# Low parts of the first keys moved behind the second minimum, and a second price for the sum of ident's rows

## The chip, the cores and the metric

The kernel runs on one core of a Trainium2 chip. The metric is the device time of one execution in microseconds (us), as the median of several runs. TensorE is called PE here, its weight load PEld, VectorE DVE, ScalarE ACT, GpSimd POOL and SyncE SP; SP issues the loads and stores.

## What is computed

Three stages follow one another: causal attention with a decay from gates, a feed-forward block with SoLU and a layer norm, and a second feed-forward block with squared relu. All arrays are float32. Shapes: 4 batches, 8 heads, 576 positions, head size 64, so 2304 tokens of width 512; inner widths 1024 and 2048.

```python
def _attn_ref(q, k, v, f):
    scores = scale * np.matmul(q, k.transpose(0, 1, 3, 2))
    cum = np.cumsum(np.log(np.clip(f, 0.0001, 1.0)), axis=-1)
    decay = cum[:, :, :, None] - cum[:, :, None, :]
    scores = np.where(causal, -1000000000.0, scores + decay)
    attn = np.exp(scores - np.max(scores, axis=-1, keepdims=True))
    attn = attn / (np.sum(attn, axis=-1, keepdims=True) + 1e-09)
    return np.matmul(attn, v)

def _moe_ref(x, w_in, w_out, g_ln):
    h = x @ w_in
    solu = h * softmax(h)
    ln = (solu - mean(solu)) / np.sqrt(var(solu) + 1e-06) * g_ln
    return ln @ w_out

def _moe2_ref(x, w_in, w_out):
    h = np.maximum(x @ w_in, 0.0)
    return h * h @ w_out
```

## The kernel before

Every product is made from high and low parts: a number is rounded to the matmul's short form (the high part), and what is missing (the low part) is a second operand. So each tile of keys, queries, sums of gates and weights costs a cast for the high part and a subtraction for the low one, on whichever of ACT, DVE and POOL the plan picks.

The attention goes over 20 tiles of up to 128 queries (tiles 0 and 1 are the first two of batch 0), and in each over 8 heads. Heads 0 to 3 take their operands from row half j = 0, heads 4 to 7 from j = 1. For one head: two matmuls give negated scores in a PSUM tile z0 or z1, in turn (line 576; the second matmul takes the low parts and the gate sums); DVE adds the causal mask and takes the row minimum (597, with a second instruction that reads it out); ACT takes the exponential (611); PE transposes it (630); ACT or DVE copies the transposed tile to `pt` (376, 382); and PE multiplies it with the values (650). A z tile is free for the head after the next only when its exponential is done.

What stands before the first minima: the gates are clipped, their logarithms are summed along the positions in two scans on DVE (1575), the sums get a high part on ACT (1606) and a low part on DVE (1609, `low_sums` in the change), and both go to DRAM (`cumd`), from where the keys' tiles fetch them as extra rows (506). Tile 0 takes its own rows straight from SBUF. Lines 510 and 498 make the high and the low part of the keys (`K1`, `K2`), 384 or 378 the scaled queries, 541 their low part. Line 482 (`picks`) fills rows of the query operand `q2` that pick a head's gate sums out of the extra rows: it adds two slices of the identity matrix `ident`, once for each of two buffers i and two halves j. Buffer i = 0 serves even tiles, i = 1 odd ones. Beside this, the weights of the first block are converted: lines 729, 380 or 378, 733, 737, 743 (a sum of whole words, on POOL alone) and 747 (their low part `wil`).

Each operation is entered as a step with `pl.add`: a price in ns for each engine that may do it, a priority (lower goes first) and the keys it reads and writes, from which the plan takes the dependences. `Plan.lay` then lays out all steps in a list by these prices, and the engines run the program in that order; nothing is reordered on the chip. A step marked `port=True` on DVE is laid so that it doesn't run while a POOL step runs, as the plan's prices have it. Up to a planned time of 140 us, gaps on PE are filled with transposes that nobody reads (1706).

Of the kernel before, what the change touches and what calls it, by code (L numbers as in the profile page):

```python
# [27 lines left out]
class Plan:  # L28
# [11 lines left out]
        dve=dict(pe=230, dve=127, act=198, pool=203, dma=1230),  # L40
        act=dict(pe=110, dve=142, act=153, pool=160, dma=1234),
        pool=dict(pe=135, dve=75, act=75, pool=88, dma=1200),
# [17 lines left out]
    def add(self, eng, fn, prio, reads=(), writes=(), take=None, uses=(), late=0, port=False, kind="r"):  # L60

        s = Step()
        s.eng, s.fn, s.prio, s.take, s.no, s.late = eng, fn, prio, take, len(self.steps), late
        deps = {}
        s.uses = tuple(uses) + ((take,) if take else ())
        for k in s.uses:  # L70
            self.users.setdefault(k, []).append(s)
        s.weak, s.port, s.kind = None, port, kind
        for k in reads:
            if k in self.writer:
                deps[self.writer[k].no] = self.writer[k]
            rs = self.readers.setdefault(k, [])
            if k in self.banks or k[0] in ("pp", "hp"):

                if rs and rs[-1].no not in deps:
                    s.weak = rs[-1]  # L80
                    deps[s.weak.no] = s.weak
            rs.append(s)
        for k in writes:
            if k in self.writer:
                deps[self.writer[k].no] = self.writer[k]
            for r in self.readers.get(k, ()):
                deps[r.no] = r
        for k in writes:
            self.writer[k] = s
            self.readers[k] = []  # L90
        deps.pop(s.no, None)
        s.deps = list(deps.values())
        s.succ = []
        for d in s.deps:
            d.succ.append(s)
        s.left = len(s.deps)
        s.rdy = {}
        s.end = None
        self.steps.append(s)
        return s  # L100

    def fill(self, order, ring, a, b, lag, share):
        ident = self.writer["ident"]
# [165 lines left out]
def tile_kernel(ctx: ExitStack, tc: tile.TileContext, q, k, v, f, w_in, w_out, g_ln, w2_in, w2_out, out):  # L269
# [23 lines left out]
    HH = H // 2  # L293
# [150 lines left out]


    vslot = {}

    def load_k(n, prio):
        T = tiles[n]
# [26 lines left out]
    def picks(i, j):  # L476

        def fn():
            c = D + HH * j
            a, b = (ident[AUX, x : x + HH].unsqueeze(2).broadcast_to([2 * H, HH, P]) for x in (c, c + H))  # L480
            eng = nc.gpsimd if s.on == "pool" else nc.vector
            eng.tensor_tensor(out=Q2[i][j][AUX], in0=a, in1=b, op=ALU.add)

        s = pl.add(dict(dve=602, pool=1252) if i else dict(dve=602), fn, -9.05e6 if i == 0 else 14000, ["ident"], [("qa", i, j)], port=True)

    def prep_k(n, prio):
        T = tiles[n]
# [3 lines left out]
        los = {}  # L491
        for j in range(2):
# [15 lines left out]
            if n == 0 and j:  # L508
# [7 lines left out]
                lo, prio + 2 * j, [("kn", j)] + hk, lk,  # L516
                port=True,
            )
            for y in range(2):
                rk = [f"cumd{y}"] if n else [("c0", 0), ("xh", 0, 0)][y : y + 1]  # L520
                pl.add(
                    dict(dma=350), lambda y=y, auxrows=auxrows: auxrows(y), (prio if n else -7e6) + 2 * j, rk,
                    writes=kcells(f"ka{y}", j, kc, kc + m),
                )

    def prep_q(n, prio):
        m = tiles[n]["m"]
        i = n % 2
        raw = QN[:, 0 : HH * m].rearrange("p (h s) -> p h s", s=m)
        for j, src in enumerate(own):  # L530
            q1, q2 = Q1[i][j], Q2[i][j]
            if n == 0 and j:
                prio = SECOND
            for rows, dst, nm in ((LO, q2, "qh"), (HI, q1, "qd")):
                copy(
                    HH * m, lambda rows=rows, dst=dst: dst[rows, :, 0:m], lambda src=src: raw[src], prio + 2 * j, ["qn"],
                    [(nm, i, j)], (), SC, False, None if n else ("act", "dve")[j:] if j else ("act",),
                )

            def lo(src=src, q1=q1, hi=(q1 if j else q2)):  # L540
                nc.vector.scalar_tensor_tensor(
                    out=q1[LO, :, 0:m], in0=raw[src], scalar=SC, in1=hi[src, :, 0:m].bitcast(F32), op0=ALU.mult,
                    op1=ALU.subtract,
                )

            pl.add(
                dict(dve=67 + 1.045 * HH * m), lo, prio + 2 * j, ["qn", ("qd" if j else "qh", i, j)], [("ql", i, j)],
                port=True,
            )


    def head(s):
# [48 lines left out]

        for y, (c, k_) in enumerate(zip(cuts, zk)):
            w = c[2] - c[1]
            pl.add(
                dict(dve=77 + 1.042 * w + 61 * y), lambda y=y, c=c: least(y, c), prio,
                ["mask"] + [sk_ + (0,)] * y, [k_, sk_ + (y,)],
            )
# [962 lines left out]
    for y, (a, e) in enumerate(((0, P), (P, S))):  # L1570
# [33 lines left out]
        ["mhalf", ("lf", 0), ("lf", 1), ("qh", 0, 0), ("qd", 0, 0)], [("st", 0, 0)],  # L1604
    )
    pl.add(dict(act=573), lambda: nc.scalar.copy(part(0), cu), THIRD, ["cu0", "cu1"], pt0[0])
    pl.add(
        dict(dve=669),
        lambda: nc.vector.tensor_tensor(out=part(1), in0=cu, in1=part(0).bitcast(F32), op=ALU.subtract), THIRD,
        ["cu0", "cu1"] + pt0[0], pt0[1],  # L1610
# [38 lines left out]
    for n in range(NQ):  # L1649
        for h in range(H):  # L1650
# [7 lines left out]
            if h == PQ and n + 1 < NQ:  # L1658
                prep_q(n + 1, when[s])
                if n + 2 < NQ:  # L1660
                    load_q(n + 2, when[s])
            head(s)
            w = 4 if n >= QUADS else 2
            if (h + 1) % w == 0:
                mix(s, w)
# [129 lines left out]
```

## Time and profile before

| | us |
|---|---|
| median of 3 runs | 810.95 |
| lowest and highest | 810.48, 811.85 |
| profiled execution, its own time | 813.03 |
| its span, first to last instruction | 811.2 |

The profile is one execution. 1.83 us of its time lie outside the span. Over the span PE is busy 97%, DVE 79%, ACT 68% and POOL 47%; the granted TensorE clock is 0.998 of its full level, 2.4 GHz. Busy time of PE includes the filling transposes, and ends of matmuls are modelled, so a busy PE is not PE at its peak. A time in a row is the start from the beginning of the span; in square brackets stands the idle time of the engine just before, and what ended it. Rows in which two instructions are grouped give the time from the first one's start to the last one's end.

### The profile page before, as it was taken

The numbers are of one execution on the slowest core, as the hardware profiler recorded it, in microseconds if no ns is written. First come the engines' busy times: TensorE is split into PE (matmuls) and PEld (weight loads), VectorE is DVE, ScalarE is ACT, GpSimd is POOL, SyncE is SP. The second block draws the span as 40 slices with busy tenths as digits, with TensorE's granted clock in tenths as the row PEclk, the third lists the DMA queues.
The fourth block names the chain that finished last, engine by engine and source line by source line (L and its number), as shares of the span: only waits on it lengthen the run. The fifth ranks groups of instructions, "written<-read, shape, count | busy, mean of one in ns | idle before, by whom it ended". The sixth has DMA issues, their size and how long they took to land.

```text
span 811.2 us, 19134 instructions
## 1 busy us (share of the span) xinstructions
PE 790.8 (97%) x6607; PEld 726.7 (90%) x6607; DVE 638.9 (79%) x1627; ACT 550.3 (68%) x1425; POOL 384.6 (47%) x520
## 2 busy tenths in 40 slices
PE   7899999999999999999999999999999999999997
PEld 6677788888888888888989999999999999999997
DVE  8788788787786667886677879779778877987777
ACT  6899998889998888898886775445335343533442
POOL 6467778666778686777757622120211121112110
PEclk9999999999999999999999999999999999999999
DMA  6644346656664555665477899696767767675401
GB/s 216 206 117 140 105 128 186 206 173 190 199 206 163 189 171 165 196 229 180 169 247 232 265 309 368 213 321 212 229 207 233 230 203 223 216 232 186 159 1 53
DMA packets 109665, 159.69 MB, mean 197 GB/s; under 512 B 12832, under 2 KB 52768, under 8 KB 109568
## 3 DMA queue, kind: packets, MB, share of 16 engines
q1 hardware_dynamic: 109280, 158.21, 60.9%
q8 instruction: 52, 0.85, 0.4%
q14 instruction: 45, 0.37, 0.2%
q10 hardware_dynamic: 288, 0.26, 0.1%
HBM read 121.65 MB, written 36.72 MB: 195 GB/s over the span
## 4 chain that ended last, share of the span: by engine, by line
PE 47%; POOL 2%; DVE 2%; issue 1%; DMA 1%; ACT 1%; DVEq 0%; POOLq 0%
PE z L1392 9%; PE pp L1392 9%; PE hp L1497 4%; PE hp L1498 4%; PE hp L1499 4%; PE z L1341 3%; PE xo L1498 2%; PE xo L1499 2%; PE xo L1497 2%; DMA w2d<-free 1%; PE pp L1498 1%; PE pp L1499 1%; PE pp L1497 1%; PE pp L820 1%; PE pp L822 1%
## 5 line engine op out<-in xcount | busy, mean ns | idle before, releaser
L611 ACT ACTIVATE adj<-z,st 64x288 f32<-64x288 f32 (+9 forms) x192 | 95.0, 498 | 17.7 <-DVE st L597 15.9
L576 PE MATMUL z<-k,q 80*64 80x288 f32 (+17 forms) x384 | 89.9, 331 | 0.2
L597 DVE CUSTOM_DVE_ANT_0 z<-z,maskb 128x128 f32<-128x128 f32 (+8 forms) x144 | 65.3, 462 | 26.8 <-PE z L576 24.8
L630 PE MATMUL pp<-ident,adj 128*128 128x128 f32 (+1 forms) x480 | 76.4, 273 | 9.2 <-ACT adj L611 8.2
L821 PE MATMUL pp<-ln,wol 128*128 128x256 f32 x288 | 80.1, 278 | 0.0
L822 PE MATMUL pp<-ln,woh 128*128 128x256 f32 x288 | 80.1, 278 | 0.0
L630 PEld LDWEIGHTS pp<-ident,adj 128*128 128x128 f32 (+1 forms) x480 | 50.7, 140 | 32.4 <-ACT adj L611 22.4
L376 ACT COPY pt<-pp 128x384 f32<-128x384 f32 (+5 forms) x167 | 67.5, 422 | 15.2 <-PE pp L630 13.7
L1153 DVE TENSOR_TENSOR k<-adj,k 128x512 fp32r<-128x512 f32 (+1 forms) x71 | 48.9, 688 | 32.5 <-POOL k L380 25.2
L743 POOL TENSOR_TENSOR free<-free 128x256 uint32<-128x256 uint32 x64 | 49.1, 772 | 33.9 <-DVE free L737 20.7
L576 PEld LDWEIGHTS z<-k,q 128*128 128x128 f32 (+3 forms) x384 | 54.9, 176 | 8.3 <-ACT adj L611 4.1
L869 PE MATMUL hp<-wih,xl 128*128 128x512 f32 x144 | 60.0, 417 | 0.8 <-ACT hp L908 0.8
L650 PE MATMUL xo<-pt,vn 128*64 128x128 f32 (+1 forms) x960 | 60.4, 268 | 0.1
L650 PEld LDWEIGHTS xo<-pt,vn 128*64 128x64 f32 x960 | 48.6, 137 | 9.4 <-issue 5.4
L870 PE MATMUL hp<-wil,xh 128*128 128x512 f32 x144 | 56.6, 393 | 0.2 <-DVE wil L747 0.2
L871 PE MATMUL hp<-wih,xh 128*128 128x512 f32 x144 | 56.8, 394 | 0.0
L1106 POOL TENSOR_TENSOR free<-free 128x256 f32<-128x256 f32 x64 | 52.5, 821 | 7.5 <-DMA w2d<-free 4.8
L821 PEld LDWEIGHTS pp<-ln,wol 128*128 128x128 f32 x288 | 54.4, 189 | 0.4
L822 PEld LDWEIGHTS pp<-ln,woh 128*128 128x128 f32 x288 | 54.1, 188 | 0.0
L1098 POOL TENSOR_TENSOR free<-free 128x256 fp32r<-128x256 f32 x63 | 50.0, 805 | 7.4 <-ACT free L376 6.9
L380 POOL TENSOR_SCALAR k<-adj 128x512 fp32r<-128x512 f32 x37 | 23.1, 624 | 63.7 <-PE xo L1499 25.7
L1392 PE MATMUL z<-wol,k 128*128 128x256 f32 x384 | 52.4, 276 | 0.0
(614 smaller groups left out, 2682.4 us busy)
## 6 DMA issues: line engine op xcount, KB each, us to landing
k<-w2u SPq DMA_DIRECT2D x96, 256.0 KB
ln<-w2u SPq DMA_DIRECT2D x96, 256.0 KB
w2u<-free SPq DMA_DIRECT2D x56, 256.0 KB
kn<-in_k_dram SPq DMA_DIRECT2D x32, 256.0 KB
free<-in_moe_w_out_dram SPq DMA_DIRECT2D x32, 256.0 KB
free<-in_moe_w_in_dram SPq DMA_DIRECT2D x32, 256.0 KB
q<-w2u SPq DMA_DIRECT2D x32, 256.0 KB
w2f<-free SPq DMA_DIRECT2D x49, 128.0 KB
```

What stands on the lines that cost most here:

```text
L376: nc.scalar.copy(dst(), src())
L576: nc.tensor.matmul(dst, lhsT=ql[0:r, p, 0:m], rhs=rhs, start=(g == 0), stop=(g == 1))
L597: nc.vector.tensor_tensor_reduce(out=z, in0=z, in1=maskb[0:m, o : o + e - a], scale=1.0, scalar=st[0:m, 0:1] if y else 3e38, op0=ALU.add, ...
L611: nc.scalar.activation(out=adj[0:m, c[1] : c[2]], in_=Z[c[0]][0:m, 0 : c[2] - c[1]], func=AF.Exp, bias=st[0:m, low : low + 1], scale=-1.0, ...
L630: nc.tensor.transpose(at(sk)[:, (c - g) * m : (c - g + 1) * m], adj[0:m, zc : zc + P], ident[0:m, 0:m])
L650: nc.tensor.matmul(XO[own[j], g // 2, off : off + m], lhsT=VN[vslot[b, c]][:, (g + j) * D : (g + j + 1) * D], rhs=PT[(s - h + g + j) % NPT ...
L821: nc.tensor.matmul(px, lhsT=wol[:, fc, w], rhs=hi, start=False, stop=False)
L822: nc.tensor.matmul(px, lhsT=woh[:, fc, w], rhs=hi, start=False, stop=(fc == KF - 1))
L869: nc.tensor.matmul(HP[:, c], lhsT=XL[i][:, cc, :], rhs=wih[:, cc, w], start=(cc == 0), stop=False)
L871: nc.tensor.matmul(HP[:, c], lhsT=XH[i][:, cc, :], rhs=wih[:, cc, w], start=False, stop=(cc == KC - 1))
L1392: nc.tensor.matmul(half(i), lhsT=l, rhs=r[:, c * TB : c * TB + TB], start=(j == start), stop=(j == 5), skip_group_check=True,)
L1497: nc.tensor.matmul(po, lhsT=gl, rhs=wh, start=(p == 0 and i in opens), stop=False, skip_group_check=True)
```

## The change

Four edits. A function `after` adds a dependence to a step that is already entered. The low part of tile 0's keys of half j = 1 and the low part of the gate sums are made to depend on the minimum of head 1 (`least_of[1, 0]`), that is, the second one. The low part of tile 0's queries of half j = 1 gets priority 9900 where it had 9902. And the price of the sum of ident's rows for buffer i = 1 on DVE goes from 602 to 1500 ns, where POOL's stays at 1252; for i = 0 it stays as it was.

```diff
+    def after(self, s, d):
+        if d not in s.deps:
+            s.deps.append(d)
+            d.succ.append(s)
+            s.left += 1
...
+    held_back, least_of = [], {}
...
-        s = pl.add(dict(dve=602, pool=1252) if i else dict(dve=602), fn, -9.05e6 if i == 0 else 14000, ["ident"], [("qa", i, j)], port=True)
+        s = pl.add(dict(dve=1500, pool=1252) if i else dict(dve=602), fn, -9.05e6 if i == 0 else 14000, ["ident"], [("qa", i, j)], port=True)
...
+            if n == 0 and j:
+                held_back.append(los[j])
...
-            pl.add(
-                dict(dve=67 + 1.045 * HH * m), lo, prio + 2 * j, ["qn", ("qd" if j else "qh", i, j)], [("ql", i, j)],
-                port=True,
+            s = pl.add(
+                dict(dve=67 + 1.045 * HH * m), lo, SECOND if n == 0 and j else prio + 2 * j,
+                ["qn", ("qd" if j else "qh", i, j)], [("ql", i, j)], port=True,
             )
...
-            pl.add(
+            least_of[s, y] = pl.add(
                 dict(dve=77 + 1.042 * w + 61 * y), lambda y=y, c=c: least(y, c), prio,
...
-    pl.add(
+    low_sums = pl.add(
         dict(dve=669),
...
             head(s)
+            if s == 1:
+                for x in held_back + [low_sums]:
+                    pl.after(x, least_of[1, 0])
```

Since the plan is laid step by step, the whole program comes out in another order, on every engine and through to its end; the three places below are at its start. The change's rows carry the line numbers of its own file, which are 6 to 12 higher (482 is 489, 498 is 505, 541 is 550, 597 is 606, 743 is 752, 747 is 756, 1609 is 1618).

DVE between the long scan and the third minimum of tile 0, before and with the change (`k21` is the low part of the keys of j = 1, `q2` and `q101` the queries of j = 1, `free` the gate sums):

```order
L498 TENSOR_TENSOR k21_8_79<-kn1_17_88,k11_46_117 64x4x128
L384 TENSOR_SCALAR q2_20_91<-qn_9_80 64x512
L1609 TENSOR_TENSOR free_21_92<-free_21_92 32x576
L597 ISA z0_121,st0_29_100<-z0_121,maskb_0_71 128x128
L597 ISA st0_29_100 128x1
L597 ISA z1_122,st1_30_101<-z1_122,maskb_0_71 128x128
L597 ISA st1_30_101 128x1
L384 TENSOR_SCALAR q101_42_113<-qn_9_80 64x512
L541 SCALAR_TENSOR_TENSOR q101_42_113<-qn_9_80,q101_42_113 64x512
L597 ISA z0_121,st2_31_102<-z0_121,maskb_0_71 128x128
```

```order
L390 TENSOR_SCALAR q2_20_91<-qn_9_80 64x512
L390 TENSOR_SCALAR q101_42_113<-qn_9_80 64x512
L550 SCALAR_TENSOR_TENSOR q101_42_113<-qn_9_80,q101_42_113 64x512
L606 ISA z0_121,st0_29_100<-z0_121,maskb_0_71 128x128
L606 ISA st0_29_100 128x1
L606 ISA z1_122,st1_30_101<-z1_122,maskb_0_71 128x128
L606 ISA st1_30_101 128x1
L1618 TENSOR_TENSOR free_21_92<-free_21_92 32x576
L505 TENSOR_TENSOR k21_8_79<-kn1_17_88,k11_46_117 64x4x128
L606 ISA z0_121,st2_31_102<-z0_121,maskb_0_71 128x128
```

The two low parts went behind the second minimum, and the second query copy with its low part came ahead of the first.

DVE from the last step of the first weight chunk (L737) to the minima of heads 4 to 7 of tile 0, before and with the change (`k20` and `k21` are here tile 1's keys, `q110` tile 1's queries):

```order
L737 SCALAR_TENSOR_TENSOR ln0_50_209<-ln0_50_209 128x512
L482 TENSOR_TENSOR q2_20_91<-ident_39_110 16x512
L597 ISA z0_121,st0_29_100<-z0_121,maskb_0_71 128x128
L597 ISA st0_29_100 128x1
L597 ISA z1_122,st1_30_101<-z1_122,maskb_0_71 128x128
L597 ISA st1_30_101 128x1
L597 ISA z0_121,st2_31_102<-z0_121,maskb_0_71 128x128
```

```order
L746 SCALAR_TENSOR_TENSOR ln0_50_209<-ln0_50_209 128x512
L505 TENSOR_TENSOR k20_7_78<-kn0_16_87,k10_45_116 64x4x128
L606 ISA z0_121,st0_29_100<-z0_121,maskb_0_71 128x128
L606 ISA st0_29_100 128x1
L606 ISA z1_122,st1_30_101<-z1_122,maskb_0_71 128x128
L606 ISA st1_30_101 128x1
L550 SCALAR_TENSOR_TENSOR q110_43_114<-qn_9_80,q2_20_91 64x512
L606 ISA z0_121,st2_31_102<-z0_121,maskb_0_71 128x128
L606 ISA st2_31_102 128x1
L505 TENSOR_TENSOR k21_8_79<-kn1_17_88,k11_46_117 64x4x128
L606 ISA z1_122,st3_32_103<-z1_122,maskb_0_71 128x128
```

The sum of ident's rows left DVE, and the low parts of tile 1's keys and queries stand between these minima.

POOL in the same stretch, before and with the change:

```order
L482 TENSOR_TENSOR q2_20_91<-ident_39_110 16x512
L380 TENSOR_SCALAR ln0_50_209<-ln0_50_209 128x512
L498 TENSOR_TENSOR k20_7_78<-kn0_16_87,k10_45_116 64x4x128
L498 TENSOR_TENSOR k21_8_79<-kn1_17_88,k11_46_117 64x4x128
L743 TENSOR_TENSOR ln0_50_209<-ln0_50_209 128x512
```

```order
L489 TENSOR_TENSOR q2_20_91<-ident_39_110 16x512
L386 TENSOR_SCALAR ln0_50_209<-ln0_50_209 128x512
L752 TENSOR_TENSOR ln0_50_209<-ln0_50_209 128x512
L756 TENSOR_TENSOR wil_4_75<-ln0_50_209,wih_3_74 128x512
L489 TENSOR_TENSOR q2_20_91<-ident_39_110 16x512
```

POOL gave away both low parts of tile 1's keys, and took the low part of the first weights and the second sum of ident's rows.

## Rows read from the trace of the kernel before

**Rows 1.** Busy us per engine by stretch, then granted clock, DMA share, GB/s.
```profile
0.00:20.00 20.00, 14.72 (x95) 12.51 (x96) 16.25 (x36) 12.26 (x33) 12.84 (x23) 1.00 0.69 216
...
40.00:100.00 60.00, 57.76 (x433) 45.47 (x433) 49.74 (x116) 58.01 (x146) 41.95 (x56) 1.00 0.41 125
...
120.00:440.00 320.00, 314.71 (x2571) 272.15 (x2572) 244.82 (x654) 275.93 (x797) 234.40 (x308) 1.00 0.61 194
440.00:811.00 371.00, 366.57 (x3202) 366.04 (x3200) 296.36 (x747) 166.92 (x348) 72.84 (x109) 1.00 0.66 215
```

**Rows 2.** Instructions of PE in order of time: start, us, line, tiles.
```profile
8.28 0.73 PE L576 MATMUL z<-k,q 128*128 128x256 f32 x4
...
14.41 0.73 PE L576 MATMUL z<-k,q 128*128 128x256 f32 x4
...
18.13 0.68 PE L630 MATMUL pp<-ident,adj 128*128 128x128 f32 x2 [1.84 <-ACT adj L611]
...
26.30 0.66 PE L676 MATMUL pp<-ident,x 128*128 128x128 f32 x4 [1.14 <-ACT x L376]
```

**Rows 3.** The same of ACT, in tile 0 and at its end.
```profile
17.62 0.37 ACT L611 ACTIVATE adj<-z,st 128x128 f32<-128x128 f32 x1 [2.40 <-DVE st L597]
...
23.08 0.37 ACT L611 ACTIVATE adj<-z,st 128x128 f32<-128x128 f32 x1
...
25.63 0.62 ACT L376 COPY x<-su 128x512 f32<-128x512 f32 x1 [0.83 <-DVE su L689]
```

**Rows 4.** The same of DVE, up to the third minimum.
```profile
5.33 0.67 DVE L498 TENSOR_TENSOR k<-kn,k 64x512 fp32r<-64x512 f32 x1
...
6.53 1.49 DVE L1575 TENSOR_TENSOR_SCAN free<-e,free 32x448 f32<-32x448 f32 x1
7.94 1.45 DVE L498 TENSOR_TENSOR k<-kn,k 64x512 fp32r<-64x512 f32 x1
9.41 0.42 DVE L384 TENSOR_SCALAR q<-qn 64x512 fp32r<-64x512 f32 x1
9.86 0.75 DVE L1609 TENSOR_TENSOR free<-free 32x576 fp32r<-32x576 f32 x1
10.54 0.28 DVE L597 CUSTOM_DVE_ANT_0 z<-z,maskb 128x128 f32<-128x128 f32 x1
...
11.62 0.69 DVE L541 SCALAR_TENSOR_TENSOR q<-qn,q 64x512 fp32r<-64x512 f32 x1
12.49 0.30 DVE L597 CUSTOM_DVE_ANT_0 z<-z,maskb 128x128 f32<-128x128 f32 x1 [0.18 <-ACT pt L376]
```

**Rows 5.** The same of POOL.
```profile
7.16 1.69 POOL L482 TENSOR_TENSOR q<-ident 16x512 fp32r<-16x512 f32 x1
...
13.57 3.03 POOL L498 TENSOR_TENSOR k<-kn,k 64x512 fp32r<-64x512 f32 x2 [0.52 <-ACT k L376]
16.57 1.72 POOL L743 TENSOR_TENSOR ln<-ln 128x512 uint32<-128x512 uint32 x1
...
23.60 1.73 POOL L743 TENSOR_TENSOR ln<-ln 128x512 uint32<-128x512 uint32 x1 [3.47 <-DVE ln L737]
```

**Rows 6.** The issue of a load by SP.
```profile
14.20 0.72 SPq L506 DMA_DIRECT2D k<-cumd  x2
```

**Rows 7.** DVE again, the sums of ident's rows and what follows.
```profile
1.83 1.38 DVE L482 TENSOR_TENSOR q<-ident 16x512 fp32r<-16x512 f32 x2 [0.98 <-POOL ident masks.py:199]
...
13.56 0.69 DVE L737 SCALAR_TENSOR_TENSOR ln<-ln 128x512 uint32<-128x512 uint32 x1
14.28 2.87 DVE L482 TENSOR_TENSOR q<-ident 16x512 fp32r<-16x512 f32 x1
17.18 0.30 DVE L597 CUSTOM_DVE_ANT_0 z<-z,maskb 128x128 f32<-128x128 f32 x1
```

**Rows 8.** DVE, the sum of a tile's row sums, twice.
```profile
24.20 1.16 DVE L671 TENSOR_SCALAR su<-su 128x8 f32<-128x8 f32 x1
...
41.85 0.17 DVE L671 TENSOR_SCALAR su<-su 128x8 f32<-128x8 f32 x1
```

## The prediction

> **What bounds the kernel now.** I first read busy time by stretch [rows 1]. From 440 us to the end PE is busy 366.57 of 371 us, and from 120 to 440 us 314.71 of 320: there PE sets the pace, and 5.3 us of idle time is all that an order of instructions can win there without touching PE's work. From 40 to 100 us ACT is busy 58.01 of 60 us and sets it. The first 20 us are different: no engine is full (ACT 12.26, PE 14.72 with its filling transposes). So a microsecond lost in the first 25 us is a late start for ACT and then for PE, and comes back at the end of the span. Since the change's own edits lie there, I then read the start in order of time, PE first.
>
> The scores of heads 0 and 1 are done at 8.28 + 0.73 = 9.01 us [rows 2], but DVE comes to the first minimum at 10.54 [rows 4]. That is the first late step, by about 1.5 us. The second is larger: the scores of heads 4 and 5 start at 14.41 [rows 2], so the first pair is done near 14.8 and its minimum could start near 15.0; it starts at 17.18, behind one sum of ident's rows that took 2.87 us [rows 7]. ACT then waits 2.40 us for it [rows 3], and PE 1.84 us for ACT [rows 2]. The third is small: at 24.20 a sum over 8 numbers takes 1.16 us where it takes 0.17 elsewhere [rows 8]; ACT waits 0.83 us behind it [rows 3] and PE 1.14 [rows 2].
>
> All three have one cause. DVE instructions that read SBUF are long while POOL runs: line 498 takes 1.45 us instead of 0.67 while POOL's line 482 runs from 7.16 to 8.85 [rows 4, 5]; line 482 takes 2.87 us instead of 1.38 / 2 = 0.69 while POOL's two low parts run from 13.57 to 16.60 [rows 5, 7]; line 671 takes 1.16 us inside POOL's sum of words from 23.60 to 25.33 [rows 5, 8]. In each the DVE instruction ends about its own free time after POOL's end.
>
> **The low parts behind the second minimum.** Before, 1.45 + 0.42 + 0.75 = 2.62 us of DVE work stand between the scan's end and the first minimum [rows 4]; 1.45 − 0.67 = 0.78 of it is the wait for POOL's line 482. The order of the change keeps that POOL instruction where it was and puts two query copies and their low part there: 0.42 + 0.42 + 0.69 = 1.53, with the same wait 2.31. The first minimum comes 0.31 us earlier, near 10.23, not at 9.0: the edit names two low parts, but another one takes their place. Behind the second minimum now stand 0.75 + 0.67 = 1.42 us where 0.42 + 0.69 = 1.11 stood, so DVE reaches the third minimum 0.31 − 0.31 = 0 earlier, where it sat idle 0.18 us before it [rows 4]. The gain is between 0 (third minimum) and 0.31 (first two); I take 0.2, since the exponentials, transposes and scores of the first two do come earlier and DVE had that 0.18 us to spare. The store of the low gate sums starts about 1 us later than at the end of 9.86 + 0.75; it is read back by a load issued at 14.20 [rows 6], some 2.6 us after, and SP's loads queued behind the store are for tile 1, whose first scores follow tile 0's row sums at 24.20 [rows 8]. I count 0, and 0.6 if that cover is short. The keys' low part of j = 1 is ready near 12.3; its first reader is the score at 14.41 [rows 2]: 0.
>
> **The sum of ident's rows.** With DVE at 1500 and POOL at 1252 the order puts it on POOL, and in its place on DVE stands one low part of tile 1's keys, 0.67 us free [rows 4]. That starts when line 737 ends, at 13.56 + 0.69 = 14.25 [rows 7], and POOL's two low parts, which held it up, are gone from POOL. So the fifth minimum starts near 15.0 instead of 17.18, and the 2.40 us that ACT waits are open. What is late next is POOL's sum of words, which also waits for line 737, starts at 14.3 to 14.9 and runs up to 1.72 us [rows 5], to 16.0 to 16.6. In the new order ACT's cast of those weights stands before the sixth exponential and waits for it: ACT is through with the fifth near 15.7, so the new wait is 0.3 to 0.9. Bounds: 2.40 − 1.72 = 0.7 where the whole sum of words is waited for, 2.4 where none of it is. I take 1.4, next to 2.40 − 0.9. The second sum of ident's rows costs POOL 1.69 us [rows 5] and is read by tile 1's heads of j = 1 only; POOL was busy 12.84 of the first 20 us [rows 1], and gives away 3.03 us: 0.
>
> The Trainium skill speaks against this edit (GPSIMD Engine Reference, section Engine selection): an addition of two inputs belongs on VectorE, being about twice as slow on GpSimd. The rows agree on the ratio, 1.69 to 0.69 us; by that rule alone the edit would cost 1.0 us of engine time, and by the row of this very instruction, 2.87 us on DVE, it saves 1.2.
>
> **The sum of the row sums at the tile's end.** In the new order it and its reciprocal stand ahead of the DVE step that releases POOL's next sum of words, so its 1.0 us of excess [rows 8] should go, and with it ACT's 0.83. Against that, the order now puts the scaling of tile 0's result ahead of tile 1's first two minima, and ACT does two more weight steps (about 0.65 each, by line 376's 0.62 in rows 3) before the copy that the scaling needs. Ends: +0.8 and −0.5; I take 0.2.
>
> **Sum.** 0.2 + 1.4 + 0.2 = 1.8 us. What each engine has to do does not shrink: some copies change engines, so ACT's 58.01 of 60 us and PE's stages stay and pass the gain on. The rest of the program is laid anew as well, and that may give or take: PE's idle time from 120 to 440 us is 5.3 us [rows 1], and I allow half of it, 2.6 us, either way, with 0 as the value since nothing in the rows tells its sign. The span of the profiled execution would go from 811.2 to 809.4 us, its time from 813.03 to 811.2. That execution is 2.1 us above the median of the runs, so the median goes from 810.95 to about 809.2.
>
> **Rivals.** First, the gain is given back before it reaches the bound stages. For it: ACT's eighth exponential stood at 23.08 [rows 3] behind ACT's own work, not behind DVE, and the new order puts more of ACT's casts in front of the later exponentials. Against it: ACT's wait of 2.40 us is the longest in the first 25 us, and work that starts earlier leaves less for later. Then about 0.3 us stay: 810.6.
>
> Second, slower: the wait for POOL only moves, and grows. In the new order DVE has two low parts of tile 1 between the minima of heads 5, 6 and 7, and POOL runs in the same stretch the sum of words, the low part of the weights and the sum of ident's rows. The rows show DVE waiting through two POOL instructions in a row, to the end of the second [rows 5, 7]. If the three ran in a row ahead of one of those low parts, it would wait 1.72 + 1.5 + 1.69 = 4.9 us (1.5 being half of 3.03), against 2.2 us of excess before: 2.7 us lost, 0.2 gained, and 813.4. It decides if the minimum of head 6 or 7 starts later than it did, beyond 19.5 us. Against it: ACT's cast stands between the first two of the three, so that POOL must pause there and let DVE in.
>
> The Trainium skill (SBUF — State Buffer, section SBUF: two separate sides) has DVE and GpSimd take turns at a shared pair of ports, held for one whole instruction, with the loser blocked. The trace agrees that the loser is blocked, but for two instructions, 2.18 us, not for what was left of the first. By that rule the second rival would cost at most one instruction, 1.72 us, less than the 2.2 us before, and the time would be about 810.3.
>
> Third, the edit doesn't do what it says: the sum left on DVE. The order rules that out; what the order does show is that the first edit's low parts are replaced by others, which the sum counts.
>
> **How the numbers follow.** 0.2% of this time is 1.6 us, about what can be told from no change. The forecast, 1.8 us earlier, has 0.45, and the first rival 0.35; the second has 0.12, and 0.08 is left for a rest of the program that comes out over 2.6 us worse, near 813. The forecast lies close to the bound of 809.3, so I give faster 0.46, same 0.36, slower 0.18. The bounds of the terms are 0.2 and 3.5 us of gain; with 2.6 us either way used in part, the range is 806.5 to 812.6.
>
> **What the profile would show.** First minimum near 10.2, fifth near 15.0 to 15.3, no DVE instruction of 2.87 us before it, ACT's wait of 2.40 us gone or under 1 us, line 671 near 0.2 us, the eighth exponential of tile 0 at 21.5 to 22.5, and tile 1's second pair of scores before 26. The prediction would be wrong if DVE's low parts between the minima of heads 5 and 7 took over 1.5 us each, if ACT's busy share from 40 to 100 us fell, or if PE's idle time after 120 us grew by more than 2 us.

## The result and the profile after

The kernel became slower, by 0.8%. Over six runs each, the median went from 811.65 us (810.48 to 811.91) to 817.68 us (815.73 to 822.49), a ratio of 1.0084 with an interval of 1.0057 to 1.0110. The forecast was 809.2. The profiled execution of after took 817.45 us with a span of 815.6 us, against 813.03 and 811.2 before. That profile of before lies above its median and that of after near it, so the traces show 4.4 us of the 6.0 that the medians differ by.

The signs that the prediction named for the start came out, the fifth minimum even 0.4 us earlier than said. DVE of after, from the first minimum to the row sums of tile 0, answers to [rows 4, 7, 8] (start, us, line, tiles, and in brackets the idle time before it):

```profile
10.32 0.30 DVE L606 CUSTOM_DVE_ANT_0 z<-z,maskb 128x128 f32<-128x128 f32 x1
...
13.37 0.69 DVE L746 SCALAR_TENSOR_TENSOR ln<-ln 128x512 uint32<-128x512 uint32 x1
13.97 0.68 DVE L505 TENSOR_TENSOR k<-kn,k 64x512 fp32r<-64x512 f32 x1
14.57 0.28 DVE L606 CUSTOM_DVE_ANT_0 z<-z,maskb 128x128 f32<-128x128 f32 x1
...
17.00 1.35 DVE L505 TENSOR_TENSOR k<-kn,k 64x512 fp32r<-64x512 f32 x1
...
21.94 0.17 DVE L680 TENSOR_SCALAR su<-su 128x8 f32<-128x8 f32 x1 [2.40 <-ACT adj L620]
```

The first minimum comes at 10.32 instead of 10.54, the fifth at 14.57 instead of 17.18, and the sum of the row sums takes 0.17 instead of 1.16 us. (The 2.40 in its brackets is DVE's own idle time there, not the wait of ACT that had the same length before.) ACT of after, against [rows 3]:

```profile
15.00 0.37 ACT L620 ACTIVATE adj<-z,st 128x128 f32<-128x128 f32 x1
...
15.83 0.62 ACT L382 CAST wih<-ln 128x512 fp32r<-128x512 f32 x1 [0.37 <-POOL ln L752]
...
21.46 0.35 ACT L620 ACTIVATE adj<-z,st 128x128 f32<-128x128 f32 x1
...
22.59 0.62 ACT L382 COPY x<-su 128x512 f32<-128x512 f32 x1
```

ACT's wait of 2.40 us is gone, one of 0.37 has come, and the eighth exponential starts at 21.46 instead of 23.08: 1.62 us gained at the end of tile 0. The ninth, the first of tile 1, starts at 26.13 instead of 27.23, so 1.10 us are left. Twenty us behind the eighth the gain is gone. POOL and then DVE of after in tile 1:

```profile
25.79 1.27 POOL L756 TENSOR_TENSOR wil<-ln,wih 128x512 fp32r<-128x512 f32 x1
27.02 3.12 POOL L505 TENSOR_TENSOR k<-kn,k 64x512 fp32r<-64x512 f32 x2
30.78 1.31 POOL L752 TENSOR_TENSOR ln1a<-ln1a 128x512 uint32<-128x512 uint32 x1 [0.63 <-DVE ln1a L746]
```

```profile
27.53 1.50 DVE L742 TENSOR_SCALAR ln1a<-ln1a 128x512 uint32<-128x512 uint32 x1
...
29.29 1.40 DVE L746 SCALAR_TENSOR_TENSOR ln1a<-ln1a 128x512 uint32<-128x512 uint32 x1
...
30.96 1.41 DVE L742 TENSOR_SCALAR ln1b<-ln1b 128x512 uint32<-128x512 uint32 x1
```

Those three take 0.4 to 0.7 us each where POOL is still. POOL now makes both low parts of tile 2's keys beside the first two, and a sum of words beside the third. The sixteenth exponential, the last of tile 1, starts at 41.28 us (40.78 before). The 1.62 us of gain have become 0.50 of loss. From there on the difference goes both ways: the seventeenth exponential is 3.07 us late, the fortieth 0.89 early and the last, of 192, 2.64 late (423.60 against 420.96); the two lists put different work between them.

Then busy time by stretch, against [rows 1] (PE, PEld, DVE, ACT, POOL, granted clock, DMA share, GB/s):

```profile
0.00:20.00 20.00, 16.16 (x94) 13.94 (x95) 15.85 (x37) 13.88 (x37) 11.35 (x23) 0.83 0.68 211
...
40.00:100.00 60.00, 58.10 (x454) 46.48 (x453) 51.43 (x118) 57.50 (x148) 39.07 (x54) 1.00 0.42 127
120.00:440.00 320.00, 313.92 (x2559) 271.67 (x2559) 243.31 (x653) 273.22 (x783) 232.63 (x312) 0.99 0.60 190
440.00:815.60 375.60, 370.52 (x3220) 369.24 (x3218) 301.65 (x756) 167.57 (x349) 76.56 (x115) 1.00 0.67 216
```

PE's idle time from 120 to 440 us is 6.1 us (5.3 before), so little is seen there; but its clock is 0.99, and 0.83 in the first 20 us. In windows of 2 us that gives two places. One is 12 to 20 us, with 0.66, 0.50, 0.50 and 0.64. The other:

```profile
122.00:124.00 2.00, 1.40 (x10) 0.78 (x9) 1.76 (x9) 1.96 (x7) 1.83 (x3) 1.00 0.31 65
124.00:126.00 2.00, 1.47 (x25) 1.31 (x26) 1.26 (x2) 1.75 (x8) 1.36 (x2) 0.82 0.39 132
126.00:128.00 2.00, 2.00 (x11) 1.43 (x12) 0.99 (x5) 1.19 (x6) 1.00 (x2) 0.50 0.62 150
128.00:130.00 2.00, 2.00 (x10) 1.66 (x11) 0.00 (x0) 1.63 (x6) 2.00 (x3) 0.50 0.94 276
130.00:132.00 2.00, 2.00 (x10) 1.82 (x9) 1.30 (x5) 1.15 (x6) 1.56 (x3) 0.50 0.92 240
132.00:134.00 2.00, 2.00 (x19) 1.56 (x19) 1.01 (x9) 0.87 (x7) 0.00 (x0) 0.98 0.94 334
```

PE is busy 1.40 and 1.47 of 2 us, and then works at 0.50, the 1.2 GHz level, for 6 us: 10 or 11 matmuls in 2 us where the window at 0.98 has 19. Before, the clock was 1.00 in all of these windows. A busy share hides this, since slow work counts as busy. What the second place costs is measured below: 2.7 us.

PE's account from 20 us on nearly closes. Rows of before that were not shown ahead, and the same two of after:

```profile
20.00:40.00 20.00, 17.10 (x133) 13.82 (x132) 15.73 (x37) 17.91 (x47) 8.62 (x8) 1.00 0.67 205
40.00:120.00 80.00, 77.73 (x614) 62.13 (x613) 65.72 (x156) 77.28 (x203) 55.90 (x75) 1.00 0.40 120
```

```profile
20.00:40.00 20.00, 16.42 (x119) 12.44 (x118) 15.05 (x32) 16.72 (x43) 11.29 (x10) 1.00 0.71 218
40.00:120.00 80.00, 78.10 (x630) 64.52 (x628) 67.83 (x156) 75.58 (x199) 53.85 (x74) 1.00 0.39 117
```

Idle before: 2.9 + 2.3 + 5.3 + 4.4 = 14.9 us; after: 3.6 + 1.9 + 6.1 + 5.1 = 16.7. That is 1.8 us more idle time, and with 2.7 us for the half clock 4.5 us, where the spans differ by 4.4. Filling transposes count as work in this, so it is an account, not a proof. It is also an account of two executions only. Among the other five of after one had a mean clock of 1.000 and a span of 814.0 us, 1.6 less than the profiled one, and took 815.73 us, still 4.1 above the median of before. So most of the loss is not the clock.

### The profile page after: what moved, and what is told of

It reads as the page before. It is cut to its first block, busy times and chain, and to the rows that moved or that the text cites. A ratio compares the mean times of both kernels' runs of the same rounds, so it can differ in the third digit from the quotient of the medians.

```text
span 815.6 us, 19144 instructions
## 1 busy us (share of the span) xinstructions
PE 795.1 (97%) x6614; PEld 731.8 (90%) x6614; DVE 643.7 (79%) x1633; ACT 547.0 (67%) x1409; POOL 385.7 (47%) x530
## 4 chain that ended last, share of the span: by engine, by line
PE 57%; DVE 4%; ACT 2%; issue 1%; DVEq 0%; ACTq 0%
PE pp L1401 9%; PE z L1401 9%; PE hp L1508 4%; PE hp L1506 4%; PE hp L1507 3%; PE z L1350 3%; PE xo L659 2%; PE pp L639 2%; PE xo L1506 2%; PE xo L1508 2%; PE pp L829 2%; PE xo L1507 2%; PE z L585 2%; PE pp L831 2%; PE pp L830 2%; PE hp L878 1%
## 5 line engine op out<-in xcount | busy, mean ns | idle before, releaser
L585 PE MATMUL z<-k,q 128*128 128x256 f32 (+17 forms) x384 | 90.9, 336 | 1.1 <-ACT adj L620 1.0
L382 ACT COPY pt<-pp 128x256 f32<-128x256 f32 (+5 forms) x168 | 67.2, 419 | 15.7 <-PE pp L639 13.8
L752 POOL TENSOR_TENSOR free<-free 128x256 uint32<-128x256 uint32 x64 | 51.3, 808 | 44.6 <-DVE free L746 35.3
L585 PEld LDWEIGHTS z<-k,q 128*128 128x128 f32 (+3 forms) x384 | 57.4, 181 | 7.3 <-ACT adj L620 2.4
L382 ACT CAST k<-adj 128x512 fp32r<-128x512 f32 (+1 forms) x34 | 21.0, 617 | 46.7 <-DVE adj L1476 30.1
```

The lines of the kernel that those rows point to most:

```text
L382: nc.scalar.copy(dst(), src())
L585: nc.tensor.matmul(dst, lhsT=ql[0:r, p, 0:m], rhs=rhs, start=(g == 0), stop=(g == 1))
```

## The experiments

Three theories, by the letters that the expectations use. Theory A: the change's own steps gain what the start shows, and the list that the plan lays anew from them loses more, since the list of before is better than one laid anew usually is. Theory B: what the start gains is taken back on the way, on any list. Theory C: the loss comes from what the change does in itself (the moved steps, the stall that came to tile 2's low parts, or the low clock). Times are medians, with the kernel before run beside each. Exponentials are counted one by one; a head of the widest tiles has two, so the forty-eighth is the last of the fortieth head. The head 16 and the head 48 of the expectations are the sixteenth and the forty-eighth exponential.

### The edits on the list of before

Only the moved steps, put by hand into the finished list of before, with nothing laid anew. First the sum of ident's rows alone:

```diff
     order = pl.lay(SLACK)
+    moved = sums[1, 1]
+    words = ...  # POOL's first sum of words behind it
+    moved.on, moved.start = "pool", words.end
+    order.sort(key=lambda s: (s.start, s.no))
```

> The list of the kernel before, with a single step changed after the plan is laid: the second sum of ident's rows (buffer 1, half 1) runs on POOL, behind the sum of words that starts at 16.57 us, instead of on DVE at 14.28. Nothing else moves. If the gain at the start reaches the end (theory A: the loss comes from the rest of the program, which the plan laid anew), this is 1 to 2.2 us faster than before, ratio 0.997 to 0.999. If the start's gain is taken back on the way (theory B), the ratio is 1.000 within 0.0007. If the move itself does the harm (theory C), it is slower by some us.

Then with the low parts behind the second minimum as well:

```diff
+    for n_, x in enumerate([low_sums] + held_back):
+        x.start = least_of[1, 0].start + 1 + n_
```

> As one_step, and the low part of tile 0's keys of half 1 and the low part of the gate sums stand behind the second minimum on DVE, again on the list of before, with nothing else moved. Theory A: the first minimum starts near 9.7 us instead of 10.54, the eighth exponential near 21.5 instead of 23.08, and the end comes 1.5 to 2.5 us earlier, ratio 0.997 to 0.998. Theory B: ratio 1.000. Theory C: slower, near the change's 1.008.

Measured: 810.51 us (809.72 to 812.19) and 810.23 us (809.06 to 811.13) beside 811.58, ratios 0.9986 (0.9973 to 1.0000) and 0.9986 (0.9974 to 0.9997). Both are faster, by 1.07 and 1.35 us; the first interval just reaches no change, the second just leaves it out, and 1.35 is less than the 1.5 to 2.5 that Theory A expected. The harm that Theory C expected is not seen. DVE of the second:

```profile
9.07 0.30 DVE L602 CUSTOM_DVE_ANT_0 z<-z,maskb 128x128 f32<-128x128 f32 x1
...
14.72 0.30 DVE L602 CUSTOM_DVE_ANT_0 z<-z,maskb 128x128 f32<-128x128 f32 x1 [0.86 <-PE z L581]
```

Without the other steps that the new plan pulls in front, the first minimum comes at 9.07, the 1.5 us that the prediction's first part had named as open. The eighth exponential comes at 21.20, 1.88 us earlier than before. The lead is 0.93 us at the sixteenth (the clock was low at 26 to 30 us, shown below), 0.87 at the fortieth and 1.64 at the last (419.32 against 420.96). In the first of the two kernels it is 0.92 at the eighth, 0.24 at the sixteenth, also behind a low clock, 0.22 at the fortieth and 1.17 at the last. That both leads grow, by 0.77 and 0.95, towards the last may lie in the profiled execution of before, which was above its median. So half of the lead or more goes in the stretch where the clock is low, and what is left at the sixteenth is carried; for that rest Theory B falls.

### The edits apart, with the list laid anew

The price alone (`dve=602` to `dve=1500` in the kernel before):

> The change's price of 1500 ns alone, planned anew. Theory A: the start gains as in the change, and the time is anywhere within some 5 us of before, since the rest is another list; it need not agree with one_step, which makes the same move on the old list. Theory C: between before and the change, near 1.004 to 1.008, as the price is the larger of the two edits at the start.

The waits alone (the kernel after, with `dve=602` and with the low part's priority as before):

> The change without the price: the two low parts depend on the second minimum, planned anew with 602 ns. Theory A: again another list, with a time within some 5 us of before that has little to do with the 0.2 us earlier first minimum. Theory C: near before, 1.000 to 1.002, since the harm would lie in the price.

Measured: 814.40 us (ratio 1.0029, 1.0017 to 1.0040) and 816.34 us (1.0059, 1.0039 to 1.0078). DVE of the first, then of the second:

```profile
15.07 2.10 DVE L498 TENSOR_TENSOR k<-kn,k 64x512 fp32r<-64x512 f32 x1 [0.83 <-ACT k L376]
17.10 0.28 DVE L597 CUSTOM_DVE_ANT_0 z<-z,maskb 128x128 f32<-128x128 f32 x1
```

```profile
14.50 0.28 DVE L606 CUSTOM_DVE_ANT_0 z<-z,maskb 128x128 f32<-128x128 f32 x1
...
14.87 1.40 DVE L489 TENSOR_TENSOR q<-ident 16x512 fp32r<-16x512 f32 x1
```

The price alone does put the sum of ident's rows on POOL, but gains nothing at the start, where the expectation had the gain of the change. A low part of tile 1's keys takes its place on DVE and waits there, while POOL makes the other low part (13.56, 1.81 us) and the sum of words (15.34, 1.28 us). The fifth minimum comes at 17.10 (17.18 before) and the eighth exponential at 23.12 (23.08). With the waits alone the sum stays on DVE, but behind the fifth minimum, which comes at 14.50; the eighth exponential comes at 20.25, 2.83 us earlier than before. So on lists laid anew the gain at the start came with the waits, not with the price. Both end later all the same, by 2.8 and 4.8 us: the size of the gain at the start says nothing about the end. Both medians lie within Theory A's 5 us and outside Theory C's ratios.

### Lists laid anew for no reason

The kernel before with prices that mean nothing, one at a time:

```diff
-        ns = dict(act=(51 if psum else 94) + ...
+        ns = dict(act=(53 if psum else 96) + ...
```

> The kernel before with no edit of the change at all: the plan counts every copy on ACT as 2 ns longer (51 to 53, 94 to 96), and lays the program anew from that. The difference of the lists has some 300 pieces on PE and 250 on DVE, as many as the change's own (324 and 301). Theory A (a newly laid list differs by itself by some us, whatever was meant) expects a time over 1.5 us away from before's 811.6, more likely above than below, 813 to 818. The rival (the list of before is no better than others, and the change's loss comes from its own edits) expects 810.5 to 812.7.

```diff
-                dict(dve=67 + 1.045 * HH * m, pool=...
+                dict(dve=72 + 1.045 * HH * m, pool=...
```

> The kernel before with no edit of the change: the plan counts the low part of a key of tiles 1 and later as 5 ns longer on DVE (67 to 72). Again the lists are laid anew, with 230 pieces of difference on PE and 282 on DVE. Theory A expects 813 to 818, and another difference than the one with 2 ns more for ACT's copies; the rival expects 810.5 to 812.7 for both.

The same two the other way round, with 49 and 92, and with 62:

> The kernel before, the plan counting every copy on ACT as 2 ns shorter (51 to 49, 94 to 92); 225 pieces of difference on PE. If any newly laid list is worse than before's, 813 to 822, with no relation to copies_2ns's 821.5; the rival (the sign decides) expects 808 to 811.

> The kernel before, the plan counting the low part of a key of tiles 1 and later as 5 ns shorter on DVE (67 to 62), the other way round than low_5ns; 228 pieces of difference on PE. If any newly laid list is worse than before's by some us (+2.8 to +10.4 so far, four lists besides the change's), 813 to 822. The rival (the sign of the tweak decides, since the two longer ones were slower) expects 808 to 811.

| list laid anew by | us | before beside it | difference |
|---|---|---|---|
| copies on ACT 2 ns longer | 821.50 | 811.13 | +10.4 |
| copies on ACT 2 ns shorter | 820.87 | 811.89 | +9.0 |
| the change | 817.68 | 811.65 | +6.0 |
| low parts 5 ns longer | 816.50 | 811.13 | +5.4 |
| the waits alone | 816.34 | 811.58 | +4.8 |
| the price alone | 814.40 | 811.58 | +2.8 |
| low parts 5 ns shorter | 812.59 | 811.89 | +0.7 |

Seven lists laid anew, four of them for no reason, are 0.7 to 10.4 us slower than the one they come from, 5.6 on the mean, and none is faster; the one with 0.7 can't be told from no change. The change's 6.0 lies in the middle of what no reason at all costs. The rival that the sign of the tweak decides fell: both signs of the copies' price cost the same. The expectations missed two of the four: 821.50 is above the 818 given, and 812.59 (ratio 1.0014, 0.9998 to 1.0030) below the 813. The places differ: with 2 ns more for the copies PE is idle 5.5 us from 40 to 120 us, against 2.3 before, with 5 ns less for the low parts 2.3. Rows of these two in that order, one for each kernel:

```profile
40.00:120.00 80.00, 74.52 (x580) 59.60 (x579) 63.65 (x155) 76.87 (x199) 55.66 (x74) 1.00 0.39 125
```

```profile
40.00:120.00 80.00, 77.68 (x615) 62.48 (x613) 65.54 (x156) 77.23 (x202) 55.94 (x75) 1.00 0.38 123
```

### Tile 2's low parts on DVE

The list of after, with these two steps moved by hand to DVE, and the loads that wait for them no earlier. The first kernel puts them behind the third spread of 1-bit words past a planned 20 us, the second behind the first past 25 us:

```diff
+    spread = ...  # DVE's spreads of 1-bit words, past 20 us (25 us in the second kernel)
+    late_ = spread[2].end          # spread[0] in the second kernel
+    for j_ in range(2):
+        low_ = low_of[2, j_]
+        low_.on, low_.start = "dve", late_ + 1 + j_
+        for y_ in low_.succ:
+            if y_.on == "dma":
+                y_.start = max(y_.start, late_ + 3 + j_)
```

> The kernel after, with the lists of after, but the two low parts of tile 2's keys (POOL at 27.02, two in 3.12 us) put on DVE behind its third spread of 1-bit words at 32.63. Three DVE instructions at 27.53, 29.29 and 30.96, that took 1.50, 1.40 and 1.41 us there, should take 0.7 each, ACT's wait of 1.26 us at 29.46 should go, and head 16's exponential should come 1.5 to 2 us earlier than in after (41.28). If this stall is what gave the start's gain back and the gain is carried on, the end comes 1 to 2 us earlier than after's 817.5, at 815.5 to 816.5; if the wait at head 48 and the low clock behind it eat it, the end stays at 817 to 818.

> As tile2_lows_on_dve (the kernel after, its lists, the two low parts of tile 2's keys on DVE instead of POOL), but put behind the minimum at 30.62 us of after's trace and so ahead of the next loads of keys, no step of SP's queue moved. The wait of 12.9 us in SP's queue for DVE's low part should be gone (under 3 us), PE should not stand nearly empty at 44 to 46 us, and head 16's exponential should come 1 to 2 us earlier than in after (41.28). If the gain there is carried to the end, 815.5 to 816.5; if the rest of after's list gives it back as it gave back the start's, 817 to 818.5.

The first took 826.69 us (818.85 to 828.36; ratio 1.0170, 1.0121 to 1.0220). Its profiled execution is the one of 818.85 us; the other three took 826.44 to 828.36 at mean clocks of 0.982 and 0.983, and no trace shows where. In the profiled one the two low parts stand later than the expectation says, behind the next spread of 1-bit words (35.12):

```profile
36.33 2.38 DVE L505 TENSOR_TENSOR k<-kn,k 64x512 fp32r<-64x512 f32 x2
```

The sixteenth exponential starts at 39.20, 2.08 us earlier than in after, of which 0.65 stands already at the eighth (20.81 against 21.46), ahead of the moved steps. But the seventeenth, the first of tile 2, comes at 46.54 where after has 44.82. In between stands a new wait, in SP's queue (engine, line, waited for: us, times, longest):

```profile
SPq L461 <- DVE k L505: 12.9, 2, 12.7
```

PE of the same kernel, when the loads behind it came late:

```profile
43.24 0.66 PE L686 MATMUL pp<-ident,x 128*128 128x128 f32 x4 [1.39 <-ACT x L382]
43.82 0.43 PE L660 MATMUL xo<-pt,vn 128*64 128x128 f32 x2
46.22 1.12 PE L660 MATMUL xo<-pt,vn 128*64 128x128 f32 x6 [1.96 <-ACT pt L382]
```

A load of keys stood ahead of all others and waited for the low part that still read its buffer; PE then stood nearly empty from 44 to 46 us. The second took 820.20 us (813.85 to 821.89; ratio 1.0086, 1.0054 to 1.0117), no better than after. Its sixteenth exponential came at 40.68, 0.60 us earlier than in after where 1 to 2 were expected, since the two low parts now stand in DVE's own way there. SP's waits for low parts on DVE were 13.3 us in three, the longest 7.0, where under 3 were expected; after has 7.5 in two with the same longest. From the eighth to the sixteenth exponential after takes 19.82 us, the first of these kernels 18.39 and the second 19.28. The stall in tile 1 is thus real and worth 0.5 to 1.4 us, too little for the change's loss, and neither kernel ends earlier by its median. Whether what its removal gains in tile 1 is carried to the end stays open, since the executions of the second kernel differ by 8 us among themselves, with mean clocks of 0.982 to 0.996. As the main cause the stall falls.

### Filling transposes

The list of after, all other work in its order, with more filling transposes:

```diff
-WARM, GAP, SHARE, FILL = 140000.0, 400.0, 0.6, 62.0
+WARM, GAP, SHARE, FILL = 140000.0, 150.0, 0.9, 62.0
```

> The kernel after, with filling transposes in each of PE's planned gaps of over 150 ns (400 in after) before 140 us, 0.9 of the gap instead of 0.6; some 110 more of them, and the order of all other work as in after. If the half clock at 12 to 18 and 125 to 132 us is what costs, the granted clock stays at 1.00 in both stretches and the time falls by 2 to 3.5 us, to 814 to 815.5. If the clock only shows an idle PE that waits anyhow, or the fillers stand in the way of PE's own work, it stays at 817 to 819.

Measured: 821.93 us (ratio 1.0145, 1.0115 to 1.0176), slower than after by 4.2. The clock stayed at 1.00 in the second stretch but was at 0.50 from 14 to 20 us again, so the first half of the expectation failed. It still separates two things, since behind the same two waits it runs the same instructions at the granted clock of 1.00. PE of after and of this kernel there:

```profile
122.59 0.93 PE L585 MATMUL z<-k,q 128*64 128x256 f32 x4 [0.55 <-ACT adj L620]
...
124.53 0.43 PE L685 MATMUL pp<-ident,x 64*128 64x64 f32 x4 [0.56 <-DVE ln1b L959]
124.89 1.05 PE L659 MATMUL xo<-pt,vn 128*64 128x64 f32 x20
```

```profile
128.34 0.93 PE L585 MATMUL z<-k,q 128*64 128x256 f32 x4 [0.55 <-ACT adj L620]
...
130.28 0.43 PE L685 MATMUL pp<-ident,x 64*128 64x64 f32 x4 [0.56 <-DVE ln1b L959]
130.64 0.80 PE L659 MATMUL xo<-pt,vn 128*64 128x64 f32 x20
```

From the forty-eighth exponential to the fifty-sixth after takes 133.80 − 122.44 = 11.36 us, this kernel 136.85 − 128.19 = 8.66: the half clock costs 2.7 us there. But at the forty-eighth it is already 5.7 us behind after: up to 125 us it has 322 filling transposes in 43.6 us where after has 215 in 30.0. The fillers stood in the way; more of them everywhere is no repair. Theory C's low clock is thus worth 2.7 us at one place of one execution. It is not the main cause: the execution of after at a mean clock of 1.000 kept 4.1 us of loss, and two executions of price_only at 1.000 took 812.66 and 812.88 us, above the 811.58 of before. The thin stretch lies over 100 us behind the change's own steps, in what was laid anew: in the traces 84 matmuls that make the first feed-forward block's inner values stand ahead of the forty-eighth exponential's scores before, 96 in after.

One place only, then, on the list of before with the change's steps (start_only). There PE idled 1.07 us ahead of the flip of the eighth head (the transposes of line 630), and the clock was low at 26 to 30 us:

```diff
         n = int((b - a) * share / FILL)
+        n += 14 if 17700 < a < 17900 else 0
```

> start_only (the list of before with the change's steps moved by hand) and 14 more filling transposes behind the 16 that stand ahead of the flip of the eighth head, where PE idled 1.07 us at 20.6. They should fit in that wait. If PE's thin stretch at 20.6 to 24.4 is what let the clock fall to 0.60 and 0.55 in 26 to 30 us there, the clock stays at 1.00, the 13 fillers at 26.54 take 1.6 instead of 2.98 us, and the end comes 0.3 to 1 us earlier than start_only's 810.2, at 809.2 to 809.9; if not, it stays at 810 to 810.6.

Measured: 809.32 us (808.30 to 811.03) beside 811.98, ratio 0.9968 (0.9957 to 0.9979): 2.7 us faster than before, and the fastest kernel here. Windows and PE of start_only, then the same of this kernel:

```profile
26.00:28.00 2.00, 2.00 (x11) 2.00 (x12) 2.00 (x6) 1.76 (x5) 1.09 (x1) 0.60 0.80 252
28.00:30.00 2.00, 2.00 (x12) 2.00 (x11) 0.76 (x3) 0.97 (x6) 0.20 (x1) 0.55 0.02 4
```

```profile
21.71 0.33 PE L635 MATMUL pp<-ident,adj 128*128 128x128 f32 x1 [1.07 <-ACT adj L616]
...
26.54 2.98 PE L1711 MATMUL pp<-ident 128*128 128x128 f32 x13
```

```profile
26.00:28.00 2.00, 1.52 (x15) 1.28 (x13) 2.00 (x7) 1.77 (x6) 1.30 (x1) 1.00 0.72 229
28.00:30.00 2.00, 2.00 (x18) 1.65 (x19) 1.38 (x5) 1.84 (x6) 0.00 (x0) 1.00 0.03 8
```

```profile
18.66 3.44 PE L1712 MATMUL pp<-ident 128*128 128x128 f32 x30
21.94 0.27 PE L636 MATMUL pp<-ident,adj 128*128 128x128 f32 x1
...
25.92 1.58 PE L1712 MATMUL pp<-ident 128*128 128x128 f32 x13
```

The idle time is filled, the clock stays at 1.00, and 13 fillers take 1.58 instead of 2.98 us. The sixteenth exponential comes at 38.34, 1.5 us earlier than in start_only, and all of it is still there at the last (417.60 against 419.32). Of the 1.5 us 0.57 stands already at the eighth (20.63 against 21.20), since a load of weights for which ACT waited 0.54 us in start_only had come in time here; the fillers don't explain that. The 0.9 behind it fits the clock, and the lead over before stays whole, 2.45 us at the eighth and 2.44 at the sixteenth. That the fillers kept the clock up is not shown, with one trace of each: before had PE busy 1.45, 1.16 and 1.05 of 2 us in the windows from 22 to 28 us, and its clock stayed at 1.00.

## Why the prediction was wrong

- **What bounds the kernel: right.** A gain at the start is passed on by the full stages. start_and_14_fillers shows it, with a lead of 2.44 us at the sixteenth exponential and 2.42 at the fortieth, and start_only with 0.93 and 0.87, once the low clock had taken its part.
- **Low parts behind the second minimum: right.** 0.31 us was worked out for the first minimum and 0.22 came; the third minimum came 0.20 earlier (12.29 against 12.49) where 0 was worked out.
- **The sum of ident's rows: right in size, not in what brings it.** 1.4 was taken out of 0.7 to 2.4. The new wait of ACT, bounded by 0.3 to 0.9, was 0.37, and the fifth exponential came 2.62 us earlier; of that and of the term before 1.62 was left at the eighth, where 0.2 + 1.4 was worked out. But the price that the prediction gave it to gained nothing at the start by itself, and the waits gained it without the price. On the old list the same move gained 0.92 us at the eighth exponential. The 1.69 us that the sum was to cost POOL is a time beside a busy DVE: it took 1.36 in after and 1.03 in one_step.
- **Row sums at the tile's end: the waits right, the sum wrong.** Line 680 takes 0.17 us, and ACT's copy comes without the wait of 0.83. But from the eighth exponential to the ninth the lead fell from 1.62 to 1.10: −0.5, the lower end of what was given, where +0.2 was taken.
- **The rest laid anew: the step that failed.** The prediction gave it the value 0 and 2.6 us either way, half of PE's idle time. That idle time bounds what an order can win; it bounds no loss, since a worse order adds idle time and slow clock that are in no row of before. Here the step cost 817.68 − 810.23 = 7.45 us against the moved steps on the old list, and seven such lists cost 0.7 to 10.4 us. The sign that "nothing in the rows tells" was in no single row, and lists that differ by nothing meant would have told it.
- **First rival (the gain is given back, 810.6): partly.** On the new list it was given back, and more; on the old one about half was, where the clock was low, and 1.35 us came by the medians. No run shows the reason named, ACT's casts ahead of later exponentials, to be what did it.
- **Second rival (the wait for POOL moves and grows, 813.4): moved, but not where it was put.** Heads 6 and 7 have their minima at 16.62 and 19.18, ahead of its 19.5. The stall came in tile 1, and undoing it gave 0.5 to 1.4 us there and no earlier end by the medians. With the price alone the wait did move as the rival says, from the sum of ident's rows to a low part, 2.10 us for 2.87, without growing. The Trainium skill (SBUF — State Buffer, section SBUF: two separate sides) has the engine that comes second blocked for the whole instruction of the other. In after the trace agrees with one instruction: DVE's 1.50 us from 27.53 end at 29.03, inside POOL's second low part, so it waited for the first and not for both. The 2.87 us of [rows 7] and price_only's 2.10 do not: there DVE waited on through the POOL instruction that followed.
- **The case of 0.08, a rest that comes out over 2.6 us worse, near 813: it is what happened,** and its chance and its size were both far too small.
- **The signs of a wrong prediction:** DVE's steps between the minima of heads 5 and 7 took 0.97 and 1.35 us, under 1.5; ACT's busy time from 40 to 100 us fell from 58.01 to 57.50; PE's idle time after 120 us grew by 1.4 us (0.8 + 0.6), under 2. Only the second pointed the right way. A sign that was missing is the granted clock.

What stays open: why the list of before is better than those laid anew. Each of the seven loses at other places, and only after's were followed. One reason that no run tests is that the list of before may itself have been the best of many; then a new one is slower on the average for that alone.

## What to carry to other kernels

Where a planner lays the whole program anew from its prices, a change of one price is two changes: the step that is meant, and a new draw for all else. Estimate the second by laying the program anew a few times with prices that differ by nothing meant; and when the step itself is wanted, move it by hand in the list that was measured. Read the granted clock by windows beside the busy share, as work at half clock looks like a full engine.

## What was not expected of the hardware

- The clock fell to 0.50 behind a thin stretch of PE: 1.1 us of idle time in 4 us, and then 2.7 us of loss. The same two waits of 0.55 and 0.56 us left it at 1.00 in another kernel, so the gap alone does not decide. The Trainium skill (TensorE: Matmul & The Clock Gate, section Part 1: The HAM clock gate) says that the warm-up at a kernel's start varies from run to run. No run here shows the warm-up by itself, but the mean clock of one kernel does vary. The six executions of after have 0.984 (822.49 us) to 1.000 (815.73 us), and the four with tile 2's low parts early 0.982 (821.89 us) to 0.996 (813.85 us). So differences of 7 to 8 us between executions go with the clock; what else differed between them is not known, and before shows no such relation (810.84 us at 0.993, 814.21 at 0.995).
- With fourteen fillers where PE had to wait anyhow the kernel took 0.9 us less by the medians (810.23 to 809.32, taken beside 811.58 and 811.98), though the executions of the two overlap, and 107 placed by a looser rule cost 4.2.
- SP's queue issues its loads in order: one load that waited 12.7 us for a DVE step held up all behind it, and PE stood nearly empty 2 us for it.
